# Three-tile loads for 21 of 32 attention heads, and wider selection, sum and spread products, in a decode block on one core

## The chip, the core and the metric

One core of a Trainium2 chip runs the whole program. The metric is the device time of an execution in microseconds, as the median of several runs. The profile shows one execution: its times count from the first instruction, and its span ends with the last. TensorE is called PE, VectorE DVE, ScalarE ACT, GpSimd POOL and SyncE SP; SP does nothing here but issue DMAs, in order.

## The reference

One decode step of a block with adaptive layer norm, in float32: 4 sequences, 512 channels, 32 query heads on 8 key-value heads, 4096 cached positions.

```python
def _A_ref(x, k_cache, v_cache, wq, wo):
    q = (x @ wq).reshape(B, Sq, Hq, Dh).transpose(0, 2, 1, 3)
    k = jnp.repeat(k_cache, rep, axis=1)          # (4, 8, 4096, 128) -> 32 heads
    v = jnp.repeat(v_cache, rep, axis=1)
    scores = jnp.einsum("bhqd,bhkd->bhqk", q, k) * (Dh ** -0.5)
    o = jnp.einsum("bhqk,bhkd->bhqd", _softmax(scores), v)
    return o.transpose(0, 2, 1, 3).reshape(B, Sq, Hq * Dh) @ wo
def _B_ref(x, w1, b1, w2, b2):                    # token mixer, one token, hidden size 1792
    h = _layernorm(x)
    u = _gelu(jnp.einsum("bsd,sf->bdf", h, w1) + b1)
    return (jnp.einsum("bdf,fs->bds", u, w2) + b2).transpose(0, 2, 1)
mod = (_silu(c) @ w_mod).reshape(c.shape[0], 6, 1, -1)
sa, ca, ga, sb, cb, gb = (mod[:, j] for j in range(6))
h = _layernorm(x) * (1 + ca) + sa
x = x + ga * _A_ref(h, k_cache, v_cache, wq, wo)
h = _layernorm(x) * (1 + cb) + sb
x = x + gb * _B_ref(h, w1, b1, w2, b2)
```

The caches are 134 of the 157 MB that are read: a key tile and a value tile of 2 MB each for every one of the 32 pairs of sequence and key-value head (called heads 0 to 31 below).

## The kernel before

Everything is issued in the order in which the code stands; waits between engines follow from the data. The caches are laid out on the host, so that a load takes one unbroken stretch of memory (a row) for each of the 128 partitions.

**Loads.** A ring of three slots of 32 KB a partition (`ring`, `bufs=3`) takes all that is read once: the first two modulation weights (`wm01`), the query weights (`wq`, two loads), the keys of heads 0 and 1 (`kk`), and then pairs. `load_pair(i)` fills a slot with the keys of head i + 2 and the values of head i, 32 KB a partition, 4 MB in all. A slot is free when both its tiles have been read. The output projection `wo` has four own buffers of two heads each, loaded one by one (`load_wo`) between the pairs; the middle modulation weights (`load_wm24`, two loads) take a slot of the ring for a while. For the last heads keys and values are loaded singly (`LK`, `LV` in the plan), the last values in pieces, and the sixth modulation weight last (`LW`).

**Rounds.** After a prologue (modulation, query projection `qs`, scores of heads 0 and 1) a loop runs rounds i = 0 to 23. Round i does the scores of head i + 2 (`scores`, PE, s), its row maximum (`row_max`, DVE, m), the selection for head i - 1 (`pick`, PE, pt: of the values product's output it keeps the rows that count) and the division by the sum (`copy_o`, DVE, oT), the transpose of head i + 1's probabilities (`turn`, DVE, p), its sums (`sums`, PE, pl), head i - 1's projection (`project`, PE, pa) and its addition (`add_up`), the maximum over the partitions for head i + 2 (`turn_max`, PE, pm; `col_max`, DVE, mx; `spread_max`, PE, pb: the negative maximum goes to all partitions; `copy_max`), the exponential (`expo`, ACT), and around the spread the two halves of the values product of head i (`values`, PE, pv), which `copy_v` takes out of PSUM. After round 2 the middle modulation is computed (`mod`). From round 8 on, a mixer for the sequence that has just been finished runs in between (`Mixer`: statistics pst, a spread phb, gelu on ACT, products py on PE). Heads 24 to 31 and the last mixers follow a hand-written `PLAN`, a string of steps.

Each round's first statement issues the next pair, so in program order the load of round i stands ahead of round i's scores; at run time SP waits there until the slot is free:

```python
    for i in range(NS - HKV):
        load_pair(i + 1)
        if i in (1, 3, 5):
            load_wo(i + 1)
        if i == 1:
            load_wm24()
        scores(i + 2)
```

The selection has four products with 4 columns each; `WIDE` makes them 96 and 128 columns wide for heads 27 and 28 by repeating the columns. Sums have one product with 4 columns, the spread one with a single column.

## Time and profile before

| | us |
|---|---|
| runs: median (lowest to highest of 3) | 386.45 (386.39 to 386.74) |
| the profiled execution: its span, first to last instruction | 384.7 |
| median less span | 1.75 |
| PE busy / DVE / ACT / POOL in the span | 298.7 / 198.2 / 112.2 / 7.7 |
| mean granted PE clock (share of full) | 0.883 |
| DMA: mean GB/s over the span, MB | 410, 157.69 |

The profile gives no other time of that execution than its span. A row of its timeline reads: start in us, duration, engine, line, operation, output tile <- inputs, shapes, and how many instructions were merged; in square brackets stands how long the engine had been idle and what ended that. PE's products in float32 are two records each. A row of its table of stretches reads: from:to, length, busy us (and instructions) of PE, PE's weight loads, DVE, ACT and POOL, the granted clock, the DMA engines' share and GB/s. The digit lines divide the span into 40 slices of 9.6 us; 9 means busy for 90% or more, and PEclk is the granted clock in tenths.

### The profile page before, as it was taken

To read this page: it belongs to the slowest core of one execution; us is meant where nothing else is said; L and a number is where in the kernel's file an instruction comes from. 1 tells how busy PE (TensorE), PEld (TensorE's weight loads), DVE (VectorE), ACT (ScalarE), POOL (GpSimd) and SP (SyncE) were. 2 spreads that over 40 slices of the span, in tenths; PEclk is the share of its full clock that TensorE was granted. 3 is DMA by queue.
4 is the path that set the end of the run, shared out by engine and by line. 5 is a ranking of instruction groups with operands and counts; after the bars stand their busy time and mean duration, and the time that the engine had idled before them with its cause. 6 is when DMAs were issued, how large, how long until landed. Compare 5 with 4: busy or idle time off the path is not lost.

```text
span 384.7 us, 5604 instructions
## 1 busy us (share of the span) xinstructions
PE 298.7 (78%) x2380; PEld 117.2 (30%) x2380; DVE 198.2 (52%) x407; ACT 112.2 (29%) x144; POOL 7.7 (2%) x33
## 2 busy tenths in 40 slices
PE   0856777866966949979877878788888887999984
PEld 0112122311323313334322222342222343333653
DVE  1130251620451424664866545557665567778757
ACT  1001111121110110212567311124575105657276
POOL 1100000000000000000000000000000000000000
PEclk9989555985695685998999998999999999999999
DMA  8999999999999999999999999999999999999930
GB/s 331 433 433 436 411 453 433 409 432 436 423 441 433 434 436 436 434 436 431 429 425 433 428 433 434 429 433 431 429 434 436 434 436 432 424 417 423 418 122 3
DMA packets 7409, 157.69 MB, mean 410 GB/s; under 512 B 964, under 2 KB 1236, under 8 KB 1496
## 3 DMA queue, kind: packets, MB, share of 16 engines
q1 hardware_dynamic: 7376, 157.33, 95.4%
q8 instruction: 18, 0.29, 0.3%
q14 instruction: 7, 0.06, 0.0%
q10 hardware_dynamic: 8, 0.00, 0.0%
HBM read 157.32 MB, written 0.01 MB: 409 GB/s over the span
## 4 chain that ended last, share of the span: by engine, by line
DMA 60%; PE 29%; DVE 7%; ACT 2%; issue 1%; POOL 0%; SPq 0%; POOLq 0%; DVEq 0%
DMA kv<-in_kv 58%; PE s L231 8%; PE pv L291 7%; PE s L122 2%; PE qs L138 2%; DVE m L236 2%; DVE p L267 2%; DMA sm<-in_small 2%; PE pa L343 2%; PE pt L328 2%; ACT uu L562 1%; PE pb L251 1%; PE pve L303 1%; PE pm L240 1%; PE pgx L348 1%
## 5 line engine op out<-in xcount | busy, mean ns | idle before, releaser
L231 PE MATMUL s<-kv,QT 128*32 128x512 f32 x512 | 75.2, 714 | 38.9 <-DMA kv<-in_kv 37.0
L236 DVE TENSOR_REDUCE m<-s 128x1 f32<-128x1024 f32 x32 | 39.2, 1224 | 96.0 <-PE s L231 95.9
L261 ACT ACTIVATE p<-s,nm 128x1024 f32<-128x1024 f32 x32 | 35.7, 1115 | 180.6 <-DVE nm L256 180.5
L291 PE MATMUL pv<-kv,p 128*32 128x512 f32 x464 | 69.8, 670 | 0.7 <-DMA kv<-in_kv 0.7
L231 PEld LDWEIGHTS s<-kv,QT 128*32 128x32 f32 x512 | 15.8, 123 | 84.0 <-DMA kv<-in_kv 52.5
L328 PEld LDWEIGHTS pt<-g,po 128*128 128x128 f32 x236 | 31.1, 205 | 27.2 <-issue 19.9
L343 PE MATMUL pa<-wo,oT 128*32 128x512 f32 x240 | 34.6, 648 | 4.6 <-DVE oT L335 4.4
L328 PE MATMUL pt<-g,po 128*128 128x4 f32 (+2 forms) x236 | 33.9, 267 | 1.5 <-DVE po L314 1.0
L267 DVE STREAM_TRANSPOSE p<-p 128x1024 f32<-128x1024 f32 x25 | 30.9, 1234 | 0.0
L314 DVE COPY po<-pv 128x512 f32<-128x512 f32 x29 | 20.0, 688 | 16.8 <-PE pv L291 16.7
L245 DVE TENSOR_REDUCE mx<-pm 1x128 f32<-1x512 f32 x32 | 21.3, 669 | 1.1 <-PE pm L240 1.1
L442 DVE TENSOR_SCALAR u<-hb,wr,sm 128x512 f32<-128x512 f32 x40 | 19.9, 541 | 1.9 <-POOL wr L437 1.0
L506 ACT ACTIVATE u<-u 128x1024 f32<-128x1024 f32 x20 | 20.4, 1051 | 1.5 <-DVE u L442 1.4
L361 DVE TENSOR_TENSOR acc<-acc,pa 128x512 f32<-128x512 f32 x26 | 17.8, 686 | 4.3 <-PE pa L343 4.2
L261 ACT ACT_TABLE_LOAD x11 | 14.1, 1283 | 20.3 <-DVE nm L256 20.2
L251 PEld LDWEIGHTS pb<-neg,mx 1*128 1x128 f32 x64 | 10.4, 202 | 28.2 <-DVE mx L245 26.5
L122 PE MATMUL s<-wm,sT 128*4 128x512 f32 x16 | 9.1, 732 | 10.6 <-DVE sT L108 10.6
L506 ACT ACT_TABLE_LOAD x13 | 16.7, 1283 | 0.2
L291 PEld LDWEIGHTS pv<-kv,p 128*32 128x32 f32 x464 | 13.4, 146 | 7.2 <-issue 3.1
L240 PE MATMUL pm<-ident,m 128*1 128x128 f32 x32 | 9.3, 289 | 7.4 <-DVE m L236 3.5
L251 PE MATMUL pb<-neg,mx 1*128 1x1 f32 x64 | 13.1, 271 | 2.1 <-DVE mx L245 2.1
L453 PE MATMUL py<-u,sm 128*32 128x512 f32 x80 | 14.4, 616 | 0.0
(158 smaller groups left out, 214.7 us busy)
## 6 DMA issues: line engine op xcount, KB each, us to landing
kv<-in_kv SPq DMA_DIRECT2D x28, 4096.0 KB, 21.9
wq<-in_wq SPq DMA_DIRECT2D x2, 4096.0 KB, 16.3
wo<-in_wo SPq DMA_DIRECT2D x4, 2048.0 KB
kv<-in_kv SPq DMA_DIRECT2D x4, 2048.0 KB, 20.3
wm<-in_wmod SPq DMA_DIRECT2D x2, 2048.0 KB, 14.8
kv<-in_kk SPq DMA_DIRECT2D x1, 4096.0 KB
kv<-in_vv SPq DMA_DIRECT2D x3, 1024.0 KB
wm<-in_wmod SPq DMA_DIRECT2D x1, 1024.0 KB
```

The costliest lines, as they stand in the source:

```text
L231: mm(s[32 * c:32 * c + 32, n * 512:(n + 1) * 512], QT[:, b, h, :], KT[i][:, (n * 4 + c) * 512:(n * 4 + c + 1) * 512], start=True, stop=True)
L236: dv.tensor_reduce(M[i], S[i], axis=AX.X, op=OP.max)
L245: dv.tensor_reduce(mx, M[i].rearrange("o (c r) -> o r c", c=4).unsqueeze(1).to_broadcast([1, 4, 32, 4]), axis=AX.X, op=OP.max)
L251: mm(pb, M[i].rearrange("o c r -> o (c r)"), neg1, start=True, stop=True)
L261: nc.scalar.activation(p, S[i], AF.Exp, bias=M.pop(i), accum_out=l)
L267: dv.transpose(PL[i][0], PL[i][0])
L291: mm(PV[i][32 * q:32 * q + 32, :], pT[:, 128 * k:128 * k + 128:4], VT[i][:, 4 * k:4 * k + 4, :].rearrange("p j d -> p (j d)"), start=(k < ...
L314: dv.tensor_copy(PV[i], pv)
L328: mm(pt, po[:, c * DH:(c + 1) * DH], sel.unsqueeze(1).to_broadcast([P, m, REP]), start=(c == 0), stop=(c == n - 1))
L343: mm(pa[32 * g:32 * g + 32, :], oT[:, g:g + 1].to_broadcast([P, 32]), wo_t[h][:, g, :], start=True, stop=True)
L442: dv.tensor_scalar(u[:, e, :], hb, wr[:, j:j + 1], b1[:, j:j + 1], op0=OP.mult, op1=OP.add)
L506: nc.scalar.activation(u, u, AF.Gelu_apprx_tanh)
```

## The change

The three slots become one buffer of six tiles of 16 KB a partition, `RING`, used in a circle, and the loads become a list (`queue`). Values 0 to 20 and keys 2 to 22 come in 14 loads of three tiles, 48 KB a partition and 6 MB each, by turns keys-values-keys (heads m + 2, m, m + 3) and values-keys-values (m + 1, m + 4, m + 2); the host lays them out so (`kvk`). From values 21 on there are pairs, and single tiles at the end as before. `wo` is one buffer loaded in two halves; the first modulation weights lie in it ahead of the first half, and the middle ones (one load of 24 KB a partition) ahead of the second half. `advance(name)` is called after a tile's last reader has been issued, and issues every load whose place has then only tiles that were read. The middle modulation is computed after round 1 instead of round 2. In rounds 0 to 23 selections and sums are 256 columns wide and spreads 96, with repeated columns of which the first are used.

```diff
-WIDE = {NS - 5: 24, NS - 4: 32}
+WIDE = {NS - 5: 24, NS - 4: 32, **{i: 64 for i in range(NS - HKV)}}
+NT = 14
+NP = NT * 3 // 2
...
-    neg1 = pad.tile([1, 96], F32, name="neg1")[:, 0:1]
+    negs = pad.tile([1, 96], F32, name="neg1")
+    neg1 = negs[:, 0:1]
...
-    wm01 = ring.tile([P, 2, 4, D], F32, name="wm01", tag="kv")
-    nc.sync.dma_start(wm01, wmod[0])
+    RING = ring.tile([P, 6, SK], F32, name="kv")
+    wo_t = wos.tile([P, HKV, REP, D], F32, name="wo")
+    wm01, wm24 = wo_t[:, 0:2], wo_t[:, 4:7]
+    nc.sync.dma_start(wm01, wm0)
...
+    def queue():
+        q = [entry(["K0", "K1"], kk)]
+        for n in range(NT):
+            m = n // 2 * 3
+            names = [f"V{m + 1}", f"K{m + 4}", f"V{m + 2}"] if n % 2 else [f"K{m + 2}", f"V{m}", f"K{m + 3}"]
+            q.append(entry(names, kvk[n]))
+        for i in range(NP, NS - 4):
+            q.append(entry([f"K{i + 2}", f"V{i}"], kv[i - NP]))
...
+        q.insert(2, ("wo", "M0", wo_t[:, 0:4], wo[0]))
+        q.insert(4, ("wo", None, wm24, wm2))
+        q.insert(6, ("wo", "M2", wo_t[:, 4:8], wo[1]))
+        return q
+
+    LOADS, at = queue(), [4]
+
+    def advance(name=None):
+        read.add(name)
+        while LOADS:
+            kind, names, *rest = LOADS[0]
+            if kind == "wo":
+                if names not in read:
+                    return
+                nc.sync.dma_start(*rest)
+            else:
+                n, p = len(names), at[0]
+                if any(h not in read for h in held[p:p + n]):
+                    return
...
+                held[p:p + n] = names
+                at[0] = (p + n) % 6
...
+                elif len(names) > 1:
+                    nc.sync.dma_start(RING[:, p:p + n], rest[0])
...
+            LOADS.pop(0)
...
     def scores(i):
...
+        advance(f"K{i}")
...
     def spread_max(i):
-        pb = ps_m.tile([P, 1], F32, name="pb", tag="m")
-        mm(pb, M[i].rearrange("o c r -> o (c r)"), neg1, start=True, stop=True)
-        M[i] = pb
+        n = 96 if i < NS - HKV else 1
+        pb = ps_m.tile([P, n], F32, name="pb", tag="m")
+        mm(pb, M[i].rearrange("o c r -> o (c r)"), negs[:, 0:n], start=True, stop=True)
+        M[i] = pb[:, 0:1]
...
     def sums(i):
-        pl = ps_m.tile([P, REP], F32, name="pl", tag="m")
-        mm(pl, PL[i][1].to_broadcast([P, P]), eight, start=True, stop=True)
-        RL[i] = pl
+        m = 64 if i < NS - HKV else 1
+        pl = ps_m.tile([P, m, REP], F32, name="pl", tag="m")
+        mm(pl, PL[i][1].to_broadcast([P, P]), eight.unsqueeze(1).to_broadcast([P, m, REP]), start=True, stop=True)
+        RL[i] = pl[:, 0]
...
     def values(i, ks):
...
+        if ks[-1] == 7:
+            advance(f"V{i}")
...
-        if i == 2:
+        if i == 1:
             for t in range(2, 5):
...
+            advance("M2")
```

The plan loses its load steps (`LP`, `LT`, `LK`, `LV`, `LW`) and is otherwise the same.

On SP, the issues behind the first keys (`kk`) up to the run of equal loads, before:

```order
L170 DMA kv<-in_kk 128x8192
L176 DMA kv<-in_kv 128x8192
L181 DMA wo_128<-in_wo 128x4096
L176 DMA kv<-in_kv 128x8192 x2
L181 DMA wo_129<-in_wo 128x4096
L185 DMA wm_337<-in_wmod 128x4096
L186 DMA wm_337<-in_wmod 128x2048
L176 DMA kv<-in_kv 128x8192 x2
L181 DMA wo_130<-in_wo 128x4096
L176 DMA kv<-in_kv 128x8192 x2
L181 DMA wo_131<-in_wo 128x4096
L176 DMA kv<-in_kv 128x8192 x21
```

And changed (128x12288 is a load of three tiles):

```order
L211 DMA kv<-in_kk 128x8192
L211 DMA kv<-in_kvk 128x12288
L193 DMA wo<-in_wo 128x8192
L211 DMA kv<-in_kvk 128x12288
L193 DMA wo<-in_wm 128x6144
L211 DMA kv<-in_kvk 128x12288
L193 DMA wo<-in_wo 128x8192
L211 DMA kv<-in_kvk 128x12288 x11
L211 DMA kv<-in_kv 128x8192 x7
```

Between the first keys and the run of equal loads thirteen issues have become six, of triples and whole halves of the weights.

On PE, round 13 (a mixer is running) before, with the semaphores that an instruction waits for in brackets; DMAHW stands for a load's landing:

```order
L231 MATMUL s_1088<-kv,QT 32x512 [waits DMAHW1_49]
L231 MATMUL s_1088<-kv,QT 32x512 x7
L328 MATMUL pt<-g_122,po 128x4 [waits DVE_49]
L328 MATMUL pt<-g_122,po 128x4 x3
L275 MATMUL pl<-g_122,l 128x4 [waits Activation_49]
L343 MATMUL pa<-wo_130,oT 32x512 [waits DVE_49]
L343 MATMUL pa<-wo_130,oT 32x512 x3
L240 MATMUL pm<-ident,m 1x128 [waits DVE_49]
L291 MATMUL pv<-kv,p 32x512 x4
L251 MATMUL pb<-neg_87,mx 128x1 [waits DVE_49]
L291 MATMUL pv<-kv,p 32x512 x4
```

And the same round of the changed kernel:

```order
L246 MATMUL s_1058<-kv,QT 32x512 x8
L350 MATMUL pt<-g_121,po 128x256 [waits DVE_49]
L350 MATMUL pt<-g_121,po 128x256 x3
L293 MATMUL pl<-g_121,l 128x256 [waits PE_49,Activation_49]
L365 MATMUL pa<-wo,oT 32x512 [waits DVE_49]
L365 MATMUL pa<-wo,oT 32x512 x3
L256 MATMUL pm<-ident,m 1x128 [waits DVE_49]
L309 MATMUL pv<-kv,p 32x512 [waits DMAHW2_49]
L309 MATMUL pv<-kv,p 32x512 x3
L268 MATMUL pb<-neg_87,mx 128x96 [waits DVE_49]
L309 MATMUL pv<-kv,p 32x512 x4
```

The wait for a landing, which stood ahead of every round's scores, stands in this round ahead of its values; in round 14 there is none, and in round 15 it stands ahead of the scores again; the selection (pt), the sums (pl) and the spread (pb) have their new widths.

More of the change, by code (lines that the diff above doesn't have):

```diff
@@ L90, in adaln_decode @@
     dv.memset(hT, 0.0)
-    wo_p = [wos.tile([P, 2, REP, D], F32, name=f"wo{h}") for h in range(0, HKV, 2)]
-    wo_t = [wo_p[h // 2][:, h % 2] for h in range(HKV)]
     prep = cst.tile([P, 4, P], F32, name="prep")
@@ L180, in load_wo @@
-    def load_wo(h):
-        nc.sync.dma_start(wo_p[h // 2], wo[h // 2])
-    def load_wm24():
-        w = ring.tile([P, 3, 4, D], F32, name="wm24", tag="kv")
-        nc.sync.dma_start(w[:, 0:2], wmod[1])
-        nc.sync.dma_start(w[:, 2], wmod[2][:, 0])
-        for e in range(3):
-            WM[2 + e] = w[:, e]
-    def load_wm5():
-        t = slots().rearrange("p s (k n) -> p (s k) n", n=D)
-        nc.sync.dma_start(t[:, 0:4], wmod[2][:, 1])
-        WM[5] = t[:, 0:4]
-        return t[:, 4:6]
@@ L196, in load_key @@
-    def load_key(t, i):
-        nc.sync.dma_start(t, kv[i - 2][:, 0])
-        key(t, i)
-    def load_v(t, i, cuts):
-        value(t, i)
-        src = (kv[i][:, 1] if i < NS - 2 else vv[i - NS + 2]).rearrange("p (j d) -> p j d", d=DH)
-        for lo, hi in zip(cuts, cuts[1:]):
-            nc.sync.dma_start(VT[i][:, lo:hi], src[:, lo:hi])
+    KT, VT, WM = {}, {}, {2 + e: wm24[:, e] for e in range(3)}
+    held, read = [("Q", 0), ("Q", 0), ("Q", 1), ("Q", 1), None, None], {None, ("Q", 0), ("Q", 1)}
@@ L552, in finish @@
     def finish(b, pg, py, hb, wr):
-        uu = ring.tile([P, 16, D], F32, name="uu", tag="kv")
+        uu = RING[:, 4:6].rearrange("p s (k n) -> p (s k) n", n=D)
         for js in ((0,), (1,), (2, 3, 4), (5, 6, 7), (8, 9, 10), (11, 12), (13,)):
```

112 lines of the change are left out of this document (55 added, 57 removed).

## The prediction

> **What bounds the kernel now.** I read the page from its slices down: who is busy all the time, then what the chain that ended last is made of.
>
> ```profile
> span 384.7 us, 5604 instructions
> PE   0856777866966949979877878788888887999984
> PEclk9989555985695685998999998999999999999999
> DMA  8999999999999999999999999999999999999930
> q1 hardware_dynamic: 7376, 157.33, 95.4%
> DMA 60%; PE 29%; DVE 7%; ACT 2%; issue 1%; POOL 0%; SPq 0%; POOLq 0%; DVEq 0%
> ```
>
> The DMA digits stand at 9 from the second slice to the 38th, and queue 1 was busy 95.4% of 384.7, 367 us: the sixteen DMA engines never pause until the inputs are in, and what follows is the computation behind the last values tile. DMA leads the chain with 60%. PE is the fullest engine, with holes, and its granted clock is about half where the digits read 5. So the time is the DMA stream plus a tail of some 17 us. The change must shorten the stream, or it leaves the time as it is; and it lengthens it wherever the queue runs empty. The next rows show how far from empty it is now: one round (one head) of the loop with its neighbours, in order of time (start, us, engine, line).
>
> ```profile
> 201.31 1.92 PE L231 MATMUL s<-kv,QT 128*32 128x512 f32 x16 [1.70 <-DMA kv<-in_kv]
> 203.16 1.06 PE L328 MATMUL pt<-g,po 128*128 128x4 f32 x8
> 203.30 1.23 DVE L236 TENSOR_REDUCE m<-s 128x1 f32<-128x1024 f32 x1 [2.56 <-PE s L231]
> 204.08 0.36 PE L275 MATMUL pl<-g,l 128*128 128x4 f32 x2
> 204.44 0.15 DVE L335 TENSOR_TENSOR oT<-pt,rl 128x4 f32<-128x4 f32 x1
> 204.51 1.24 DVE L267 STREAM_TRANSPOSE p<-p 128x1024 f32<-128x1024 f32 x1
> 206.07 1.10 PE L291 MATMUL pv<-kv,p 128*32 128x512 f32 x8
> 207.11 0.38 PE L251 MATMUL pb<-neg,mx 1*128 1x1 f32 x2
> 208.33 1.04 PE L453 MATMUL py<-u,sm 128*32 128x512 f32 x8
> 208.57 0.33 SPq L176 DMA_DIRECT2D kv<-in_kv  x1
> 210.98 1.06 PE L231 MATMUL s<-kv,QT 128*32 128x512 f32 x8 [1.60 <-DMA kv<-in_kv]
> kv<-in_kv SPq DMA_DIRECT2D x28, 4096.0 KB, 21.9
> ```
>
> A pair (4 MB) lands every 210.98 - 201.31 = 9.67 us. SP issues the load that reuses its slot 208.57 - 201.31 = 7.26 us after it landed, when the values product has read it; PE is through at 209.37, 8.06 us after, and waits 1.60 us. That load lands 21.9 us after its issue, though its own transfer takes 9.67: it stood more than 12 us in the queue. These 12 us are what the change spends.
>
> **The loads.** The bytes are the same. What falls is the number of rows (one partition's stretch of one load, 8 per DMA engine and load): 21 pairs become 14 triples, 168 to 112 rows per DMA engine; wo goes from four loads to two, 32 to 16; the middle modulation weights from 16 to 8. That is 80 rows fewer, and a row's fixed price is not shown. Bounds from two stretches and two landings:
>
> ```profile
> 0.00:9.60 9.60, 0.00 (x0) 0.00 (x0) 1.42 (x3) 1.50 (x2) 1.40 (x15) 1.00 0.87 332
> 9.60:19.20 9.60, 8.60 (x16) 1.49 (x16) 1.19 (x4) 0.00 (x0) 1.62 (x8) 1.00 1.00 434
> 200.00:300.00 100.00, 79.04 (x622) 30.80 (x622) 59.93 (x114) 39.72 (x46) 1.31 (x3) 0.98 1.00 432
> 329.00:349.00 20.00, 18.74 (x151) 8.46 (x153) 15.92 (x33) 11.82 (x14) 0.00 (x0) 1.00 0.99 422
> 319.02 1.10 PE L291 MATMUL pv<-kv,p 128*32 128x512 f32 x8 [0.52 <-DMA kv<-in_kv]
> 343.17 1.92 PE L231 MATMUL s<-kv,QT 128*32 128x512 f32 x16 [0.60 <-DMA kv<-in_kv]
> ```
>
> The last number is GB/s. Rows of 32 KB alone run at 432 (200 to 300 us), a stretch of mostly 16 KB rows at 422. If that whole difference were a price per row, 32 KB at 432/16 GB/s is 1.214 us, 16 KB at 422/16 is 0.621, and 2 x 0.621 - 1.214 = 0.029 us a row: 80 rows give 2.3 us, the upper end. The landings say less: from the pair that releases the values at 319.02 to the keys of head 30 at 343.17 are 24.15 us, which carry two pairs (19.34) and one 16 KB tile, so 4.81 for that tile, against 4.835 for half a pair: nothing, the lower end. I take 0.4 us, near the landings, because they measure what PE waits for. The last landings still set the end: of the rows below, head 30's values, awaited at 362.58, and the last piece of head 31, at 367.23, so what the stream saves up to there shows in full.
>
> ```profile
> 362.58 0.81 PEld L303 LDWEIGHTS pve<-kv,p 128*32 128x32 f32 x32 [0.86 <-DMA kv<-in_vv]
> 367.23 0.14 PEld L303 LDWEIGHTS pve<-kv,p 128*32 128x32 f32 x4 [0.17 <-DMA kv<-in_vv]
> 356.10 0.97 PEld L328 LDWEIGHTS pt<-g,po 128*128 128x128 f32 x8
> 356.11 1.16 PE L328 MATMUL pt<-g,po 128*128 128x128 f32 x8
> ```
>
> The Trainium skill (DMA: Bandwidth & Descriptors, "Anatomy of one DMA") gives each DMA of its software path about 2 us fixed beside bytes at 436 GB/s; were that paid by every load here, ten loads fewer would be worth 20 us. The trace disagrees: by it a pair takes 11.6 us, and lands every 9.67, so behind a full queue the fixed part is hidden, and the sum goes by the landings.
>
> **The wide products** (24 rounds each). A selection's eight passes with 4 columns take 1.06 us; the existing 128-column form, last row above, takes 1.16, and its weight loads alone 0.97. For 256 columns the lower end is that 1.16; the upper end adds weight load and stream, 8 x (0.12 + 0.24) = 2.9, where 0.24 is half of a 512-column pass (1.92 us for 16 of them, four at a time). I take the stream alone, 8 x 0.24 = 1.9: 0.85 more. All of it delays the transpose, since oT starts when the selection ends (204.22) and the maximum (204.53), both at their limit. The sums go from 0.36 to about 0.6, beside the 1.24 us transpose; the spread with 96 columns stays at its weight loads, 0.38. PE's 7.7 us a round becomes 8.8, still under 9.67: the slower landings cover it, and without that cover it would cost 1.1 us a round.
>
> **The shorter queue.** Two triples fill the ring, so a triple must be read to its last tile while the other is in transfer, 1.5 x 9.67 = 14.5 us. A restart from an empty queue takes about 1.5 us: the first slice moved 332 against 434, 2.26 us lost, 0.7 of it before the first issue. So the release has to come within 13.0 us of the landing.
> - Triple key-value-key: one round, 8.06 + 0.85 = 8.9, then the next head's scores, 1.95: 10.9. Margin 2.1 us.
> - Triple value-key-value: the values part of a round (206.07 to 209.37, 3.3), then 7.26 + 0.85: 11.4. Margin 1.6 us; 1.0 where the mixer's statistics and spread (about 0.6 us net) lie in it.
> - Before: two pairs queued, 19.3 - 1.5 - 7.26 = 10.6 us.
>
> These hold at full clock. Half clock is the unknown, and the next rows bound it:
>
> ```profile
> 136.96 1.09 PE L291 MATMUL pv<-kv,p 128*32 128x512 f32 x8
> 130.88 1.89 PE L231 MATMUL s<-kv,QT 128*32 128x512 f32 x16
> 143.25 3.64 PE L231 MATMUL s<-kv,QT 128*32 128x512 f32 x16 [5.20 <-DMA kv<-in_kv]
> 146.82 1.87 PE L328 MATMUL pt<-g,po 128*128 128x4 f32 x8
> 155.02 1.89 PE L231 MATMUL s<-kv,QT 128*32 128x512 f32 x16
> 230.47 3.26 PE L231 MATMUL s<-kv,QT 128*32 128x512 f32 x16 [2.46 <-DMA kv<-in_kv]
> 82.51 1.47 PE L215 MATMUL pm<-wm,sT 128*32 128x512 f32 x8 [2.49 <-DMA wm<-in_wmod]
> 92.21 0.66 PE L221 MATMUL pc<-ym,g 128*32 128x128 f32 x8 [0.78 <-ACT ym L218]
> 33.53 14.31 SPq L176 DMA_DIRECT2D kv<-in_kv  x2
> ```
>
> A wait of 2.46 us was followed by one slow scores step, 1.34 us more; a wait of 5.20 by a whole slow round, 143.25 to 155.02, 11.8 against 7.2 (130.88 to 138.05): 4.6 more. Per 29 us the new order leaves PE idle 29 - 3 x 8.9 = 2.3 us with a mixer, but 29 - 3 x 8.0 = 5.0 in rounds 3 to 7, which have none, and all in one place, ahead of the key-value-key triple. There the release is at 10.0 + 1.34 = 11.3 at best and 10.0 + 4.6 = 14.6 at worst: 0 to 1.6 us of empty queue each time, for two or three triples, 0 to 4.8. The Trainium skill (TensorE: Matmul & The Clock Gate, "Part 1: The HAM clock gate") says that a window of about 3.4 us with PE busy releases the clock; the slow stretches agree in that they end after dense products. By it, wide products that fill the selection's time end a slow stretch sooner, and the sum is at the best end. No row shows this for 256 columns; I take 0.3 us for all drains.
>
> **The start and the end.** The first modulation weights now lie in wo's buffer, so the first keys are issued right away instead of at 19.7 us; that is worth nothing, since the DMA engines are busy with wq then. The first triple waits for all of wq to be read, 33.53 (the row above), when the first keys are still in transfer until 37.9: 2.9 us of margin. The modulation now waits after round 1; its 10.4 us (82.51 to 92.87) start when those weights land: behind the first keys at 37.9 come two triples, 4 MB of wo and 3 MB, 20 MB at 432, so at 84 or 85. Round 2 then starts near 95 and frees the next slot at 105 to 107, while the queue (another triple, another 4 MB) lasts to 108.5: about even; this is inside the 0.3. From head 21 on pairs come again, in the old order, and slots are freed tile by tile instead of by pairs: earlier issues into a full queue, worth nothing. The memset of 96 columns instead of one stands on POOL's way to the first products:
>
> ```profile
> 9.09 0.20 POOL L68 MEMSET ones<- 128x128 f32 x1
> 9.23 0.09 POOL L69 MEMSET neg<- 1x1 f32 x1
> ```
>
> It takes between the 0.09 us of the one and the 0.20 of the other; at most 0.1 us comes off the 2.9 just named.
>
> **Sum.** -0.4 + 0.3 = -0.1. The profiled execution's span of 384.7 becomes 384.6; the median of the runs, 386.45, lies 1.75 above the span for what stands outside it, which stays: 386.3.
>
> **Rivals.**
> - Slower, by half clock: if the wide products do not shorten slow rounds, three releases at 1.6 us late, and each values triple behind them late too, give 2 to 5 us: 388 to 391. It decides where a triple is released more than 13.0 us after landing. For it: the wait of 5.20 and its 11.8 us round. Against it: only two or three triples are so placed.
> - Slower, by dear selections: at 2.9 us each the release is 11.9 and 12.4, still inside, but PE needs 7.7 + 2.1 = 9.8 us a round against 9.67, and with a mixer in 15 rounds that is 2 us, with some drains: 387.3 to 389.5. Against it: the 128-column row, where weight loads overlap.
> - Faster: the row price at its upper end, 2.3 us, without drains: 384.2. Against it: the landing of the 16 KB tile.
> - The loads don't do what is said: if a 48 KB row is cut up, the triples save nothing; 386.5.
>
> **Chances.** Queue nearly full, 386.0 to 386.7: 0.48. Half clock: 0.26. Dear selections: 0.10. Row price: 0.12 (384.2 to 385.6). Rows cut: 0.04. A difference under 0.2%, 0.77 us, can't be told from none: so faster 0.12, same 0.52, slower 0.36. The range leaves out the far ends of the first and third rivals: 385.2 to 389.5; the likeliest case alone has 386.0 to 386.7.
>
> **What would show it.** Right: DMA digits without a hole, triples landing every 14.4 to 14.5 us, SP's issues 11 to 12 us after the landing, selections near 1.9 us, PEclk digits of 9 after the first quarter. Wrong: a slice under 425 GB/s between 100 and 300 us, or scores waiting for a triple that was issued after the other landed; then half clock (PEclk 5 there) or long selections tell which. A landing gap of 14.3 or less would mean that rows cost more than I took.

## The result

| | us |
|---|---|
| before, median (range of 4 runs) | 386.45 (386.39 to 386.74) |
| after, median (range of 4 runs) | 403.28 (402.04 to 406.01) |
| after / before, with 95% interval | 1.0443 (1.0417 to 1.047) |
| profiled execution after: its time, its span | 402.86, 401.1 |

The ratios, here and below, leave out executions that took over 1.5% longer than the fastest of the same kernel. The change costs 16.8 us; the prediction had said 386.3 and at most 389.5. The DMA digits and the GB/s of the 40 slices after, then the GB/s of before (its slices are 9.6 us):

```profile
DMA  8999999999999899998999989989999999999900
GB/s 321 441 444 423 462 413 441 409 455 422 395 428 431 355 446 413 407 446 320 402 380 417 448 329 413 446 319 426 425 430 435 433 435 427 423 427 422 397 14 5
```
```profile
GB/s 331 433 433 436 411 453 433 409 432 436 423 441 433 434 436 436 434 436 431 429 425 433 428 433 434 429 433 431 429 434 436 434 436 432 424 417 423 418 122 3
```

The DMA digits now have holes, and the slices of 10 us between 130 and 280 us swing between 319 and 448 GB/s, where before none fell under 425. That is the sign that the prediction had named for being wrong. The bytes are the same (157.33 MB).

How much of the loss lies in the stream and how much behind it is read from the last load (the sixth modulation weight): the line that issues it, in before and then in after, with the time from issue to landing.

```profile
L192 SPq DMA_DIRECT2D kv<-in_wmod x1: 327/327/327, 357.8 to 357.8; - x1
DMA to landing us min/median/max: 12.3/12.3/12.3
```
```profile
L209 SPq DMA_DIRECT2D kv<-in_wm x1: 328/328/328, 370.3 to 370.3; - x1
DMA to landing us min/median/max: 12.3/12.3/12.3
```

Before, the stream ends at 357.8 + 12.3 = 370.1, and 14.6 us later the span does. After, it ends at 382.6, and 18.5 us later the span does. So of 16.4 us of span 12.5 are lost by the loads and 3.9 behind them: two costs, for which the prediction had 0.3 us and nothing.

**The loads.** The timeline of after shows each triple at three points: when SP issues it, when PE stops waiting for it (the engine's wait is in brackets), and when SP issues the next load into its slots.

```profile
139.51 3.22 PE L246 MATMUL s<-kv,QT 128*32 128x512 f32 x16 [2.08 <-DMA kv<-in_kvk]
151.17 0.33 SPq L211 DMA_DIRECT2D kv<-in_kvk  x1
171.01 3.64 PE L246 MATMUL s<-kv,QT 128*32 128x512 f32 x16 [4.66 <-DMA kv<-in_kvk]
184.41 0.33 SPq L211 DMA_DIRECT2D kv<-in_kvk  x1
200.94 0.33 SPq L211 DMA_DIRECT2D kv<-in_kvk  x1
202.03 1.92 PE L246 MATMUL s<-kv,QT 128*32 128x512 f32 x16 [0.30 <-DMA kv<-in_kvk]
213.26 0.33 SPq L211 DMA_DIRECT2D kv<-in_kvk  x1
219.06 1.10 PE L309 MATMUL pv<-kv,p 128*32 128x512 f32 x8 [1.88 <-DMA kv<-in_kvk]
232.57 0.33 SPq L211 DMA_DIRECT2D kv<-in_kvk  x1
250.94 1.61 PE L309 MATMUL pv<-kv,p 128*32 128x512 f32 x8 [2.23 <-DMA kv<-in_kvk]
```

A key-value-key triple (its first reader is s) seen at 202.03 is released at 213.26, 11.2 us later, at full clock (s takes 1.92); one seen at 171.01, whose scores ran at half clock (3.64), at 184.41, 13.4 later. A value-key-value triple (its first reader is pv) seen at 219.06 is released at 232.57, 13.5 later. Loads issued at 151.17, 184.41, 200.94 and 232.57 are seen 19.8, 17.6, 18.1 and 18.4 us after their issue. Behind a full queue a pair of before landed 21.9 us after its issue, though it needs only 9.67 for itself; a triple needs 14.5. So these loads come into a queue with almost nothing in it. A triple seen at 139.51 is followed by the next of its kind at 171.01, and that by one at 202.03: 31 to 31.5 us for two triples, where the bytes take 29.

Not every triple is late. Against 433 GB/s the low slices between 130 and 271 us (10 us each), with 355, 320, 380, 329 and 319, lost 1.8, 2.6, 1.2, 2.4 and 2.6 us: 10.7 of the 12.5, counted roughly. They hold SP's issues at 137.49, 184.41, 200.94, 232.57 and 264.16. Those at 151.17, 213.26 and 244.78 stand in slices of 413, 417 and 413, 0.5 us or less. Triples alternate, and a load takes the place of one of its own kind: four of the five late issues, all but 184.41, waited for a value-key-value place, and the three on time, like 184.41, for a key-value-key place. The place of the triple seen at 202.03 came free 11.2 us later and yet in time, since the other triple had been issued late, at 200.94, and was not due until 219.06.

**Behind the loads.** The chain of work that ended last, in order of time (start, us, what), over one whole round of after, from the scores of one head to those of the next:

```profile
295.36 1.72 PE s L246 x16
297.08 1.93 PE pt L350 x8
299.01 0.86 PE pl L293 x2
299.87 1.04 PE pa L365 x8
300.93 0.69 DVE acc L383
301.62 0.60 DVE mx L261
302.26 0.46 PE pb L268 x2
302.72 1.02 PE pv L309 x8
303.74 0.86 PE py L475 x8
304.60 1.72 PE s L246 x16
```

One round is now 9.24 us of work, one step behind the other, with no load in it; the round quoted of before took 8.06. The new selection (pt) is 1.93. The sums (pl) are 0.86, and they are on the chain: the projection (pa) stands behind them on PE, its addition (acc) waits for pa, and the maximum (mx) stands behind acc on DVE, the spread (pb) behind mx. The last wait for a triple that shows in the chain is this one:

```profile
244.78 20.44 DMA kv<-in_kvk
265.27 3.48 PE s L246 x16
```

From there to the end no load stands in the chain, which runs mostly over PE and DVE. With pairs landing every 9.68 us a round of 9.24 regains only 0.44 us of a delay; a round of 8.06 regained 1.6.

### The profile page after: what moved, and what is told of

Same layout as the page of the kernel before. It is cut to its first block, busy times and chain, and to the rows that moved or that the text cites. A ratio compares the mean times of both kernels' runs of the same rounds, so it can differ in the third digit from the quotient of the medians.

```text
span 401.1 us, 5594 instructions
## 1 busy us (share of the span) xinstructions
PE 324.9 (81%) x2380; PEld 130.4 (33%) x2380; DVE 200.6 (50%) x407; ACT 112.3 (28%) x144; POOL 7.8 (2%) x33
## 3 DMA queue, kind: packets, MB, share of 16 engines
q1 hardware_dynamic: 5936, 157.33, 92.6%
## 4 chain that ended last, share of the span: by engine, by line
PE 46%; DMA 39%; DVE 9%; ACT 2%; issue 1%; SPq 1%; POOL 0%; POOLq 0%; ACTq 0%
DMA kv<-in_kvk 21%; PE s L246 12%; DMA wo<-in_wm 10%; DMA kv<-in_kk 9%; PE pt L350 8%; PE pv L309 7%; PE pa L365 5%; PE pl L293 3%; PE py L475 3%; DVE mx L261 2%; DVE acc L383 2%; PE pb L268 2%; PE pm L230 1%; ACT kv L584 1%; PE pve L323 1%
## 5 line engine op out<-in xcount | busy, mean ns | idle before, releaser
L309 PE MATMUL pv<-kv,p 128*32 128x512 f32 x464 | 68.7, 661 | 20.0 <-DMA kv<-in_kvk 20.0
L246 PE MATMUL s<-kv,QT 128*32 128x512 f32 x512 | 71.1, 673 | 12.8 <-DMA kv<-in_kvk 12.1
L350 PE MATMUL pt<-g,po 128*128 128x256 f32 (+3 forms) x236 | 55.0, 372 | 1.4 <-DVE po L336 0.8
L350 PEld LDWEIGHTS pt<-g,po 128*128 128x128 f32 x236 | 40.5, 192 | 29.4 <-DVE po L336 11.5
L246 PEld LDWEIGHTS s<-kv,QT 128*32 128x32 f32 x512 | 16.8, 121 | 52.6 <-issue 35.0
L365 PE MATMUL pa<-wo,oT 128*32 128x512 f32 x240 | 31.8, 603 | 0.5 <-DVE oT L357 0.3
L293 PE MATMUL pl<-g,l 128*128 128x256 f32 (+1 forms) x64 | 27.9, 521 | 0.2 <-ACT p L278 0.2
L273 DVE COPY nm<-pb 128x1 f32<-128x1 f32 x32 | 5.0, 156 | 37.6 <-PE pb L268 37.5
L383 DVE TENSOR_TENSOR acc<-acc,pa 128x512 f32<-128x512 f32 x26 | 17.8, 686 | 10.8 <-PE pa L365 10.7
L309 PEld LDWEIGHTS pv<-kv,p 128*32 128x32 f32 x464 | 13.4, 146 | 28.1 <-DMA kv<-in_kvk 20.8
L528 ACT ACTIVATE u<-u 128x1024 f32<-128x1024 f32 x20 | 20.5, 1052 | 2.5 <-DVE u L464 2.3
L268 PE MATMUL pb<-neg,mx 1*128 1x96 f32 (+1 forms) x64 | 15.1, 315 | 5.7 <-DVE mx L261 5.7
L124 PE MATMUL s<-wo,sT 128*4 128x512 f32 x16 | 9.7, 775 | 10.5 <-DVE sT L110 10.5
## 6 DMA issues: line engine op xcount, KB each, us to landing
kv<-in_kv SPq DMA_DIRECT2D x7, 4096.0 KB, 16.4
```

What stands on the lines that cost most here:

```text
L246: mm(s[32 * c:32 * c + 32, n * 512:(n + 1) * 512], QT[:, b, h, :], KT[i][:, (n * 4 + c) * 512:(n * 4 + c + 1) * 512], start=True, stop=True)
L268: mm(pb, M[i].rearrange("o c r -> o (c r)"), negs[:, 0:n], start=True, stop=True)
L293: mm(pl, PL[i][1].to_broadcast([P, P]), eight.unsqueeze(1).to_broadcast([P, m, REP]), start=True, stop=True)
L309: mm(PV[i][32 * q:32 * q + 32, :], pT[:, 128 * k:128 * k + 128:4], VT[i][:, 4 * k:4 * k + 4, :].rearrange("p j d -> p (j d)"), start=(k < ...
L350: mm(pt, po[:, c * DH:(c + 1) * DH], sel.unsqueeze(1).to_broadcast([P, m, REP]), start=(c == 0), stop=(c == n - 1))
L365: mm(pa[32 * g:32 * g + 32, :], oT[:, g:g + 1].to_broadcast([P, 32]), wo_t[:, h, g, :], start=True, stop=True)
```

## The experiments

Two theories stood at first. **Short queue**: only two triples fit the ring, and a load that meets an almost empty queue lands later than its transfer takes, whatever PE does. **Wide rounds**: the longer rounds alone make everything late. All ratios are to before, timed beside it on the same chip.

### Each half of the change alone

Loads alone: the changed kernel with the old products.

```diff
-WIDE = {NS - 5: 24, NS - 4: 32, **{i: 64 for i in range(NS - HKV)}}
+WIDE = {NS - 5: 24, NS - 4: 32}
...
-        n = 96 if i < NS - HKV else 1
+        n = 1
...
-        m = 64 if i < NS - HKV else 1
+        m = 1
```

> The changed kernel with selections, sums and spreads back at their old widths; the three-tile loads stay. Short-queue theory: only two triples fit the ring, and a load that is issued when the queue has run empty lands some 2.7 us later than its transfer time (in the changed kernel one issued at 200.94 us was waited for until 219.06), so a release later than about 11.4 us after the landing leaves the DMA engines idle. Narrow rounds release at 10.0 to 10.6 us at full clock, but leave PE idle for some 5 us in every 29, so the clock falls and the release slips to 11.3 to 14.6: still slower than before, 390 to 404 us, with holes in the DMA digits. Wide-rounds theory: the longer rounds alone made the kernel slow, and without them it is back at 386 to 387 us with no hole.

Wide products alone: the same three lines the other way, in the kernel before, with the row of minus ones that a wide spread needs.

> The kernel before, with only the wide selections, sums and spreads of rounds 0 to 23. Short-queue theory: with two more pairs queued (12 us) a round of 9.2 us against a pair every 9.7 us leaves the queue full: 386.2 to 387.5 us, DMA digits 9 throughout. Wide-rounds theory: PE is late from round to round and stays so to the end: 390 us or more.

Loads alone: 401.23 us (397.12 to 405.29; the profile shows the longest of these), ratio 1.0345 (1.0289 to 1.0401). Wide alone: 387.16 us, ratio 1.0012 (1.0 to 1.0025). The loads alone bring most of the loss, and the wide products behind pairs cost about 0.6 us. Together they cost more than both added (4.4% against 3.45% + 0.12%), although the interval of the loads alone reaches up to 4.0%. The granted clock of loads alone, then of wide alone:

```profile
PEclk9969777555695966957977975978999989899999
```
```profile
PEclk9989558998796988999999999999999999999999
```

With narrow products and triples the clock falls again and again up to 280 us (0.835 on average, 0.850 to 0.856 in the three other executions; 0.902 to 0.926 for the whole change). With wide products and pairs the clock is nearly full after the first third (0.941 on average; 0.883 in the profile of before, 0.863 to 0.929 in the executions beside it), and the time doesn't fall, since the loads set it.

### Pairs, wide and narrow

The rest of the change (weights in fewer loads, the tile ring) with no triple:

```diff
-NT = 14
+NT = 0
```

> The changed kernel with no triples: all heads come in pairs through the same six-tile buffer, everything else (wide products, wo in halves, modulation after round 1, slots freed by tile) as changed. Short-queue theory: three pairs fit the ring, so 386 to 388 us. Wide-rounds theory: 390 us or more, as for the wide products alone. If the weights in halves or the earlier modulation were the cause: about 400 us as well.

> The run with pairs only, with the old narrow products too: the control for the rest of the change (one buffer, loads issued by tile, wo in halves, modulation after round 1). Both theories: 386 to 387 us. Above 390 would mean that the rest of the change costs the time.

Wide 392.0 us, 1.0145 (1.0114 to 1.0176); narrow 388.25, 1.0047 (1.003 to 1.0064). Both have one hole, in the ninth slice, and none later; GB/s of wide and then of narrow:

```profile
GB/s 326 429 429 434 429 439 429 456 230 420 432 427 432 427 429 436 434 436 431 432 428 439 428 436 427 436 434 426 431 432 432 431 432 428 422 431 423 412 60 4
```
```profile
GB/s 329 434 434 432 434 434 408 460 334 431 434 429 434 436 431 434 432 434 432 434 433 434 433 434 432 434 432 431 434 432 434 432 434 433 417 424 419 419 109 4
```

There SP waits for the second half of wo, whose buffer holds the middle modulation weights until the modulation after round 1 is through, and the next pair stands behind it. Measured against 433, the slice of 9.8 us lost 4.6 us wide and 2.2 narrow. So with pairs this part of the change costs 1.7 us by itself (388.25 less 386.57, the median of before beside it), and the holes after 130 us belong to the triples. Both runs lie above the 386 to 388 and 386 to 387 of the short queue theory, which had left that hole out. Wide products cost 3.7 us here and not 0.6; 2.4 of them are the larger hole.

### Room for three triples

Nine tiles in the ring instead of six. The room comes from leaving out work: three quarters of wo and the middle modulation load are not read (9.4 MB, 21.8 us at 432 GB/s), and the products read what lies in the quarter that is left. The control has the same left out and six tiles. Of nine against six:

```diff
-    RING = ring.tile([P, 6, SK], F32, name="kv")
+    RING = ring.tile([P, 9, SK], F32, name="kv")
...
-                at[0] = (p + n) % 6
+                at[0] = (p + n) % 9
```

> The changed kernel with room for three triples: the buffer has nine tiles, paid for by leaving out three quarters of wo (heads 2 to 7 use the weights of heads 0 and 1) and the load of the middle modulation weights (wo's bytes stand in for them). That leaves out 9.4 MB, 21.8 us at 432 GB/s. Triples and wide products are as changed. Short-queue theory: with one more triple queued no release is late, the DMA digits have no hole, and the time is that of the kernel before less 21.8: 365 to 368 us. Wide-rounds theory: the rounds are as long as in the changed kernel, so 403.3 - 21.8 = 381.5 us, 379 to 384.

> The control for the nine tiles: the same parts left out, but the six tiles of the changed kernel. Both theories: the changed kernel less 21.8 us, 381.5, between 378 and 384, with the holes in the DMA digits. Were it near 366 as well, the weights that are left out, and not the room, would have been the cause.

Nine tiles: 372.36 us (371.44 to 372.82). Six: 392.83 (392.0 to 395.22). The room is worth 20.5 us; besides it only two places in the ring that the end of the program writes to have moved. The DMA digits of nine, then GB/s of six:

```profile
DMA  8999989999999999999999999999999999999300
```
```profile
GB/s 325 428 432 478 403 450 407 473 251 161 413 457 343 467 412 393 452 283 472 314 417 462 188 401 463 341 401 423 438 433 427 435 428 424 425 427 421 361 3 3
```

That fits the short queue, but both expectations missed the sizes. The control is slower than the 378 to 384 that both theories gave: slices nine and ten (251 and 161 GB/s) lost some 10 us, in the place where the middle modulation weights and the second half of wo fill the queue in the changed kernel. So about half of the 20.5 us lies there, and not among the later triples. And nine tiles end 4 us above the 365 to 368 of the short queue theory although the stream is nearly whole. Its last load, and that of the next experiment, show why:

```profile
L207 SPq DMA_DIRECT2D kv<-in_wm x1: 328/328/328, 335.4 to 335.4; - x1
DMA to landing us min/median/max: 12.3/12.3/12.3
```

It lands at 347.7, 22.4 us ahead of before, as the bytes left out say. The span ends at 370.9, 23.2 us later, not 14.6.

### The same room, narrow products

Nine tiles as above with the old widths, to see whether the rounds are what is late.

> Room for three triples as in e5_nine_tiles, the same weights left out (9.4 MB), but with the old narrow selections, sums and spreads. In e5 the last load landed at 347.35 us, 22.3 us ahead of before, and the end came 23.6 us behind it against 15.0 in before. Theory (a wide round takes 9.24 us of PE and DVE because project and the maximum stand behind the sums, and without cover from the loads that lateness of about 8.5 us is what shows): with narrow products the end comes about 15.5 us behind the last landing, span 363, median 363.5 to 366. Rival (e5 ends late because fewer weight tiles and the mixer hold it up, whatever the width): 370 to 373.

365.96 us (365.58 to 368.86), as this theory expected. Its DMA digits and its last load:

```profile
DMA  8999999999999999999999999999999999999900
```
```profile
L207 SPq DMA_DIRECT2D kv<-in_wm x1: 327/327/327, 335.5 to 335.5; - x1
DMA to landing us min/median/max: 12.4/12.4/12.4
```

The stream ends at 347.9 as with wide products (347.7), the span (364.4) 16.5 us later instead of 23.2. So wide rounds cost 6.4 us (372.36 less 365.96) where the loads no longer cover them. And triples as such are not slow: with a third one in the queue not one slice has a hole.

### The restart, by itself

A kernel with loads only: 24 loads of 2 MB, 12 of 4 MB and 8 of 6 MB from a full queue (rows of 16, 32 and 48 KB), then four of each size one by one, each into the buffer that the one before has just filled, so that it is issued when that has landed.

> All computation is left out: 24 key tiles as 16 KB rows, the same as 32 KB rows, the same as 48 KB rows, each behind a full queue, then four loads of each size one by one, each issued when the one before has landed. Prediction's price of a row (0.005 us): 4.86, 9.68 and 14.5 us a load behind a full queue; its upper end (0.029 us): 4.97, 9.71 and 14.45. Restart: the prediction had 1.5 us over the transfer for a load that meets an empty queue; the changed kernel's landings say 2.7, so 7.5, 12.4 and 17.2 us one by one.

The rates of the three full stretches (start:end, us, POOL busy, PE clock, DMA share, GB/s), then the loads one by one, issue to landing:

```profile
20.00:95.00 75.00, 0.00 (x0) 1.00 1.01 429
120.00:205.00 85.00, 0.00 (x0) 1.00 1.00 432
240.00:335.00 95.00, 0.00 (x0) 1.00 1.01 436
```
```profile
L27 SPq DMA_DIRECT2D kv<-in_k x4: 327/328/328, 381.8 to 418.5; - x4
DMA to landing us min/median/max: 12.1/12.3/12.3
```
```profile
L29 SPq DMA_DIRECT2D kv<-in_k x4: 327/328/328, 430.8 to 483.5; - x4
DMA to landing us min/median/max: 17.4/17.6/17.8
```

From a full queue SP issues a load each time an earlier one has landed: every 4.89 us for 2 MB, 9.71 for 4 MB and 14.53 for 6 MB (at 310.34 and 324.87, for instance), which is 433 GB/s; the 436 of the row is a little high. One by one 2 MB land after 7.6 us, 4 MB after 12.3, 6 MB after 17.6. So a load that meets an empty queue pays 2.6 to 3.1 us, as the short queue theory has it. By that a triple must be released at the latest 14.5 - 3.1 = 11.4 us after its landing, and not the 13.0 of the prediction; the last experiment shows that 11.4 is still too late. From 16 to 48 KB a row the rate rises by about 1%: two loads of 2 MB take 0.07 us longer than one of 4 MB, with 8 rows more on each DMA engine, so about 0.01 us a row. Most of the kernel's bytes were in rows of 32 KB already.

### Less wide, and for fewer rounds

Wide products in rounds 0 to 17 only, and selections and sums of 128 columns instead of 256 throughout:

```diff
-        m = 64 if i < NS - HKV else 1
+        m = 64 if i < 18 else 1
```

> The changed kernel with the wide products in rounds 0 to 17 only; rounds 18 to 23 have the old widths. In the changed kernel the chain from 265 us to the end is PE and DVE work without a wait for a load, and 18.8 us pass between the last landing (382.3) and the end against 15.0 before. If that is lateness of the wide rounds 18 to 23, worth 1.2 us each, narrow ones make it up: 399 to 401 us. If all of the loss is in empty queues, which end with the last triple: 402.5 to 404 us.

```diff
-        m = 64 if i < NS - HKV else 1
+        m = 32 if i < NS - HKV else 1
```

> The changed kernel with selections and sums of 128 columns instead of 256 (spreads stay at 96). A round loses about 1.1 us on PE (8 passes 0.12 us shorter, 2 of them in the sums), the release of a value-key-value triple comes at about 11.8 us after its landing instead of 12.8, and that of key-value-key at about 10.3 instead of 11.4. Theory (a release must come about 10.5 to 11 us after a landing; drains grow with the round): drains fall from 13.8 to 6 to 11 us, the lateness of 3.7 us at the end goes, 392 to 398. Rival (half clock decides: whatever is less dense than 256 columns lets the clock fall in the waits, as in e1_loads_alone): 399 to 403.

(The table `WIDE` and, in the first, the spread are changed alike.) Up to round 17: 400.04 us (398.94 to 400.79), ratio 1.0341, as expected of lateness at the end: about 3.2 us go when the last rounds are short, and the span (397.1) ends 15.2 us after the last landing (369.5 + 12.4) instead of 18.5. With 128 columns: 398.1 us (396.54 to 399.34), ratio 1.0294, just above the range of the theory and below the rival's. Again it is the part behind the loads that went: the last load was issued at 368.5, landed 12.4 us later at 380.9, and the span of 396.3 ends 15.4 us after that instead of 18.5. The loads lost 10.8 us instead of 12.5, at a lower mean clock (0.875). So shorter rounds alone do not fill the queue.

### Holding the clock up

The value-key-value release shown above holds a slow step, so the clock's share could not be read from it. Eight products of 512 columns were added ahead of the scores of heads 8, 11, 14, 17 and 20, which wait for a key-value-key triple; the scores then overwrite their output.

```diff
+        if i in (8, 11, 14, 17, 20):
+            for n in range(8):
+                mm(s[32 * (n % 4):32 * (n % 4) + 32, n // 4 * 512:(n // 4 + 1) * 512], QT[:, b, h, :],
+                   wo_t[:, 0, 0, :], start=True, stop=True)
```

> e8_width_128 with work added: ahead of the scores of heads 8, 11, 14, 17 and 20, which wait for a key-value-key triple, PE runs eight more products of 512 columns (about 1.9 us at full clock) on weights that lie ready, into the scores' PSUM tile, which the scores then overwrite. PE has some 3 to 4 us per two triples to spare there. e8 had a mean clock of 0.875, 398.1 us, and about 11 us of empty queue. Half clock theory (waits before the key-value-key triple let the clock fall, and the slow steps after it make the releases late): the clock rises to 0.9 or more, the empty queue falls to 3 to 8 us, 390 to 396. Rival (the order alone is too tight, at any clock): the products only delay releases, 398 to 402.

> e1_loads_alone (narrow products, clock 0.835, 401.2 us, about 18 us of empty queue) with the same five groups of eight added products of 512 columns. Half clock theory: the clock rises to 0.88 or more, the empty queue falls to 8 to 13 us, 391 to 397. Rival (the order alone is too tight): 400 to 405.

With 128 columns 399.47 us (397.68 to 403.21) against 398.1 without; with narrow products 399.51 (398.33 to 400.45) against 401.23, at the same ratio as without (1.0345). Neither reached the 390 to 397 of the half clock theory. But the clock had only half been held. In the narrow kernel PE waits for both kinds of triple:

```profile
153.28 1.94 PE L313 MATMUL pv<-kv,p 128*32 128x512 f32 x8 [2.97 <-DMA kv<-in_kvk]
168.18 1.92 PE L250 MATMUL s<-kv,QT 128*32 128x512 f32 x16 [0.47 <-DMA kv<-in_kvk]
```

The scores behind the added work run at full clock (1.92). The values products (pv, 1.10 at full clock) still follow a bare wait, and run at 1.94. So the same was done ahead of the values of heads 4, 7, 10, 13, 16 and 19: with eight products in both places, with twelve ahead of the values alone, and with eight and twelve. All three have narrow products.

```diff
+            if i in (4, 7, 10, 13, 16, 19):
+                for n in range(8):
+                    mm(PV[i][32 * (n % 4):32 * (n % 4) + 32, :], QT[:, 0, 0, :], wo_t[:, 0, 0, :], start=True, stop=True)
```

> e11_narrow_filled with eight more products of 512 columns (1.9 us) ahead of the values of heads 4, 7, 10, 13, 16 and 19, which wait for value-key-value triples; the values product then overwrites their output. e11 has first values products of 1.94 us (half clock) after waits of 2.6 to 7.8 us. If half clock makes the releases late (full clock: 11.2 and about 11.7 us against a limit of 11.4): scores at 1.92 and values at 1.1 us throughout, mean clock 0.92 or more, the loads lose 2 to 6 us, 388 to 395. If the order is too tight at any clock: the clock rises and the loads still lose 9 us or more, 397 to 403.

> e1_loads_alone with twelve products of 512 columns ahead of the values of the same six heads, and none ahead of scores. Half clock theory: those values run at full clock, the scores after a wait do not, in part; clock 0.88 to 0.92, 393 to 399. Order theory: 400 to 404.

> The kernel of e12_narrow_both once more, for a profile. Half clock theory: 391 to 395 us; scores at 1.92 and first values products at 1.1 us after nearly all waits, mean clock 0.90 to 0.92, the loads lose 4 to 7 us against 18 in e1_loads_alone. If it was chance: 397 to 402.

> e14 with twelve instead of eight products ahead of the values of the six heads. Two triples take 29 us, three rounds 24.2 and the added work now 4.8: no slack is left. Half clock theory: what is won by the clock is given back, 392 to 397. Rival (more added work, fewer slow steps, less lost): 388 to 391.

Both places, eight each: 391.43, 393.92 and 394.27 us the first time (a fourth execution took 1516 us, with PE busy for 98% of it, and is left out; its cause is open) and 396.67 (394.16 to 398.45) the second, ratios 1.0176 (1.014 to 1.0212) and 1.026 (1.0211 to 1.0308). The second missed the 391 to 395 of its theory, and lies short of the 397 of chance. Values alone: 398.76 (396.2 to 401.97), at the upper edge of the half clock theory's range, but with a ratio of 1.0347 (1.029 to 1.0405) no better than loads alone. Eight and twelve: 395.07 (391.68 to 397.78), ratio 1.0169 (1.013 to 1.0207), in its range. The last of these, some rows of its timeline (waits of PE and issues of SP) and its last load:

```profile
170.25 1.92 PE L250 MATMUL s<-kv,QT 128*32 128x512 f32 x16 [1.71 <-DMA kv<-in_kvk]
186.41 1.09 PE L316 MATMUL pv<-kv,p 128*32 128x512 f32 x8 [1.05 <-DMA kv<-in_kvk]
197.46 0.33 SPq L211 DMA_DIRECT2D kv<-in_kvk  x1
200.89 1.92 PE L250 MATMUL s<-kv,QT 128*32 128x512 f32 x16 [0.94 <-DMA kv<-in_kvk]
217.21 1.09 PE L316 MATMUL pv<-kv,p 128*32 128x512 f32 x8 [0.91 <-DMA kv<-in_kvk]
227.55 0.33 SPq L211 DMA_DIRECT2D kv<-in_kvk  x1
231.71 1.92 PE L250 MATMUL s<-kv,QT 128*32 128x512 f32 x16 [0.40 <-DMA kv<-in_kvk]
262.45 3.61 PE L250 MATMUL s<-kv,QT 128*32 128x512 f32 x16 [2.57 <-DMA kv<-in_kvk]
```
```profile
L209 SPq DMA_DIRECT2D kv<-in_wm x1: 328/328/328, 366.4 to 366.4; - x1
DMA to landing us min/median/max: 12.4/12.4/12.4
```

From 166 to 250 us every step runs at full clock here, and PE still waits for every triple: two triples take 30.6, 30.8 and 30.7 us (170.25, 200.89, 231.71, 262.45) instead of 29, and the last load lands at 378.8, 8.7 us later than in before. Outside that stretch half clock is left: a wait of 2.57 us is still followed by scores of 3.61.

So of the 3.45% that triples with narrow products cost (13.3 us), work that only keeps PE busy gave back 3.3 to 6.8 us (3.45% less 1.76, 2.6 and 1.69), although it takes PE time itself. It did so only where it stood ahead of both kinds of triple; in one place alone the ratios show no gain (1.0345 and 1.0347). Nothing else was changed, so that part is put down to half clock. The intervals of the ratios of two of these three runs lie below that of the loads alone, that of one overlaps it, and the same kernel gave 1.76% once and 2.6% the other time, so the size is rough.

The rest is the order itself. The two value-key-value places above came free 11.05 us (186.41 to 197.46) and 10.34 us (217.21 to 227.55) after their landings, inside the 11.4, and 3.4 and 4.2 us ahead of the other triple's landing, more than the 3.1 of a restart; still the next two triples took 1.8 and 1.7 us too long. So the limit taken from single loads is too wide. How early is early enough no run measures; it is more than 4.2 us ahead. By an estimate, 1.6 to 1.8 us for each of the five value-key-value loads that follow 130 us make 8 to 9 us, which is about the 8.7 that are lost. Both theories have their share, and the one feeds the other: in the changed kernel a late load made PE wait 4.66 us, the scores behind the wait (171.01) ran at half clock, and the place came free 13.4 us on, so that the load issued at 184.41 was late too.

## Why the prediction was wrong

The step that failed is the shorter queue: a limit of 13.0 us for the release, with room to spare at full clock, and so "0.3 us for all drains"; 12.5 us were lost. Beside it the sum has nothing for the longer rounds, which cost 3.9 us behind the loads.

- **The restart was mis-sized, and with it the limit.** "About 1.5 us" came from the first slice, as its lost bytes less 0.7 us; measured, it is 3.1 us for 6 MB from issue to landing, and a triple issued 4.2 us ahead of the other's landing still came late. The chain of before could have told of the first part: there the second load, a small one issued at 1.18 us, lands 7.60 us later. Ahead of it stand 2 MB of modulation weights, 4.9 us at 432 GB/s, so 2.7 us or more are the start.

```profile
1.18 7.60 DMA sm<-in_small
```

With 3.1 the limit becomes 11.4 instead of 13.0 us, and margins of 2.1, 1.6 and 1.0 us become 0.5, 0 and less than 0. With the lead that the last run shows to be too short (14.5 - 4.2 = 10.3) none is left.

- **The releases were nearly right at full clock:** 10.9 was forecast for key-value-key, and 11.2 measured. At half clock 13.4 was measured, inside the forecast of 11.3 to 14.6. For value-key-value 11.4 was forecast, 12.0 with a mixer; the row shows 13.5, with a round of 9.24 us in it and not 8.9, and part of it at half clock (the second pv took 1.86). At full clock, with narrow products, it was 10.3 to 11.1.
- **"0.3 us for all drains" was 12.5, and mostly at the other triple.** Drains were put in two or three places in rounds 3 to 7, where a key-value-key triple is released late. Measured, they go on up to 271 us, and four of the five large ones wait for a value-key-value place, the one with the smaller margin. The one large drain of the forecast's kind is that behind the wait of 4.66 us (2.6 us).
- **The rival "slower, by half clock" named a true mechanism, mis-sized** (388 to 391). It counted three late key-value-key releases and the values triples behind them, and it took the order at full clock to be safe; at full clock two triples still took 1.6 to 1.8 us too long. The sign named for it all but shows: at 200.94 SP issues a load, and PE stops waiting for the other triple at 202.03.
- **The sums "beside the 1.24 us transpose"** failed. They take 0.86 us instead of 0.6 and lie on the chain through pa, acc and mx. The round became 9.24 against a forecast of 8.9. The selection itself was right: 1.9 forecast, 1.93 to 2.00 measured at full clock, where weight loads and products overlap. "Dear selections" at 2.9 is refuted.
- **"The slower landings cover it" held only while PE was on time.** With the loads of before wide products cost 0.6 us. After late triples they cost 3.9 us at the end, and 6.4 with room for three: the uncovered price that the prediction had named (1.1 us a round), and then not put into the sum for the case of a drain.
- **The start:** round 2's release was called "about even". SP issues into the place that it frees at 105.30, within the forecast, and the slice that holds it has 395 GB/s, 0.9 us lost: somewhat late. The hole that pairs have beside the modulation (ninth slice, 334 GB/s narrow) does not show with triples (455 in the changed kernel).
- **The row price was small:** about 0.01 us a row, so some 0.7 us for 80 rows against 0.4 taken. Faster by rows (384.2) had little to stand on: triples with a full queue land every 14.53 us, 1.5 times 9.69. "Rows cut" was no part of the loss, since triples with a full queue run at full rate.
- **The rule on the clock.** The prediction weighed the Trainium skill (TensorE: Matmul & The Clock Gate, "Part 1: The HAM clock gate"): by it about 3.4 us with PE busy release the clock. From that the prediction drew that dense products end a slow stretch sooner. The runs agree in direction: wide products behind pairs raised the mean clock to between 0.932 and 0.942 (before: between 0.863 and 0.929), and behind triples to between 0.902 and 0.926 (narrow: between 0.835 and 0.856). Behind pairs that gave back no time, since PE did not set it; behind triples the added dense work of the last experiments did. Where the work was missing, the step after a wait of 2.97 us took 1.94 instead of 1.10, and that after 4.66 us 3.64 instead of 1.92.

## What to carry to other kernels

Larger loads in the same room mean fewer of them in the queue: before counting what a load saves, work out when its whole buffer is free again, and compare that with the other loads' transfer less the measured price of a load that meets an empty queue. Take that price from a load that stands alone in the trace, issue to landing, not from the mean rate of a slice, and leave more room than that: here a lead of 4.2 us over the other load's landing was not enough, with a price of 3.1. Do it for each kind of load; the one with the latest reader decides. A longer step that "is covered by the loads" is only covered while the engine is on time; what it costs uncovered belongs in the sum of every case in which the loads get late.

## What was not expected of the hardware

- A single load of 4 or 6 MB is 2.6 to 3.1 us dearer than behind a full queue, and the price grows little with the size (7.6 us against 4.9 for 2 MB, 12.3 against 9.7, 17.6 against 14.5).
- Two buffers are enough for the full rate when each is issued again as soon as its load has landed (6 MB every 14.53 us, 433 GB/s). What cost 12.5 us here was a reader that kept each buffer 11 to 13.5 us.
- A load issued 3.4 to 4.2 us ahead of the landing of the one before it, longer than a restart costs, still left two triples 1.7 to 1.8 us late.
- Products added for no other purpose than to keep PE busy in its waits made a kernel faster by 3.3 to 6.8 us when they filled both kinds of wait, and by nothing that shows when they filled one.
- A mean clock of 0.947 goes with 372 us and one of 0.889 with 366 us at the same bytes (nine tiles, wide and narrow): a higher clock need not mean a shorter time.
